# Fifth pair's q' and k' turned by the DMA crossbar, the loads behind them held back, and the first weights gated on an earlier k, in a gated-attention and MLP kernel on one core

## The chip, the cores and the metric

The kernel runs on one core of a Trainium2 chip. The metric is device time in microseconds. A change of 0.5% here is 0.86 us.

The engines are called as in the profile: PE (TensorE; PEld is its weight load), DVE (VectorE), ACT (ScalarE), POOL (GpSimd) and SP (SyncE). SP, ACT and POOL each issue DMAs on a queue of their own; a "q" behind the engine's name (SPq) marks its sequencer.

## The reference

Two layers, one behind the other. The first is a gated linear attention, a recurrence over time for each of 4 x 8 heads of width 48. The second is an MLP on all 3072 tokens.

```python
B, H, S, D = 4, 8, 768, 48
for t in range(S):
    state = alpha[:, :, t, :, None] * state + np.einsum('bhd,bhe->bhde', k[:, :, t], v[:, :, t])
    y[:, :, t] = np.einsum('bhd,bhde->bhe', q[:, :, t], state)
x = y.transpose(0, 2, 1, 3).reshape(B * S, H * D)       # 3072 x 384
h = x @ w_in                                            # 384 -> 2048
g = 0.5 * h * (1.0 + np.tanh(c * (h + 0.044715 * h ** 3)))
out = g @ w_out                                         # 2048 -> 384, float32
```

## The kernel before, in words

**Tiling.** The sequence is cut into 6 chunks of 128 tokens. A unit is one chunk of one batch entry (all 8 heads); two units of one chunk make a pair. There are 12 pairs, numbered 0 to 11 in the order of work (two pairs for each chunk), so the "fifth pair" is pair 4, chunk 2.

**Attention of a pair.** `ln` (ACT) takes the logarithm of alpha, `cum` (PE) sums it along the chunk by a triangular matrix, `b` and `binv` (ACT) are exp of the sum and of its negative. `qp` and `kp` (DVE) scale q and k to q' and k'. Both have to be turned (tokens against features) into the tile `qkT`, called T below. `attn` (PE) forms k' against q', and from pair 4 on also the product of q' with the carried state. `mask` (DVE, four for a pair) keeps the lower triangle, `y` (PE) multiplies by v, `x` (ACT or DVE) copies the result out of PSUM, and x is turned as well, into `xT`. `kv` (PE) and `st` (DVE) carry the state to the next chunk; `rows` and `end` (DVE) prepare its decay.

**Turning.** There are three ways. Pairs 0 to 2 use PE transposes of whole tiles (`t`, L488) and copies out of PSUM (`ev`). The pairs in `ROWS_64` use 32 half-size PE transposes in `turn_halves` (task `t3.0` or `t4.0`, L519) and two DVE or ACT copies of PSUM in `turned_half` (`ev`, L526). The pairs in `TURN_QK` use two DMA transposes through the crossbar that SP issues in `turn_dma` (L546; tasks `turnN.0` for q' and `turnN.1` for k'). From pair 6 on x is turned by SP too (`turn_x_dma`, L552, task `turnN.2`).

**MLP.** `l1m.n` (PE, L684) is an eighth of the first layer for pair m: 6 products of 128x128 by 128x256. `gelu` follows on ACT. `l2m.n` (PE, L703) is a quarter of the second layer for one unit: 4 products with 384 columns. `ot` copies the result out of PSUM, `store` (SP) writes it. PSUM buffers are few: two banks for `yk` (turning, y, kv), four for `ff` (idle products, l1, l2), one pair for `ca`.

**Order.** Every engine runs its instructions in the order in which they were recorded. The first 45 us or so of that order are written out by hand in `FIRST` (P is PE, V DVE, A ACT, G POOL, S SP). The rest is set by a planner (`Scheduler.order`) from its own costs `W` and priorities, nudged by `SHIFT` (priorities) and `AFTER` (extra dependencies). `LANDED` tells the planner when it is to expect the early loads. None of these numbers is a wait in the program; they only decide the order.

**Loads.** The alpha, q and k of pairs 0 and 1 come in twelve loads of one unit each (`RINGS`), numbered load.0 to load.11, on SP's queue, but for those numbered in `BY_ACT`, which ACT issues: load.0 and load.1 are alpha of pair 0 (first and second unit), load.2 and load.3 are q and k of its first unit, load.4 and load.5 q and k of its second. All else is loaded by POOL in the order of `LOADS`: `v0` is v of pair 0, `in 0` to `in 3` the quarters of the first layer's weights, `out n` those of the second, `a6` alpha of pair 6, and a bare number all four of a pair. POOL loads cast to bf16 where needed, and run with several in flight.

**Gates.** A step `gatea 0 1` in `LOADS` is a tiny POOL copy (L343) that reads alpha of pair 0, unit 1, so POOL, and all loads listed behind it, wait until that load has landed. A step `hold k 5` is a POOL copy (L351) that reads T of pair 5, k' half, so the loads behind it wait until the crossbar has delivered it.

```python
def wait(self, r, m, j):
    u = self.p[list(self.p)[m]]
    return lambda e: self.nc.gpsimd.tensor_copy(self.gate[:, 0:1], u[r][:, j, 0, 0:1])
...
t = self.xT[c % self.NX][:, 2 * i + 1, 0, 0:1] if n == "x" else self.p[c, i]["T"][:, "qk".index(n), 0, 0, 0:1]
self.nc.gpsimd.tensor_copy(self.gate[:, 0:1], t)
```

`fill` tasks are products of zeros on PE (L318), put into the opening, seven of them before the first `cum`.

## Time and profile before

| | us |
|---|---|
| time, median of 3 runs | 172.98 (172.68 to 173.5) |
| time of the profiled execution | 173.12 |
| its span | 171.3 |
| outside the span | 1.8 |
| PE busy | 165.6 (97%) |
| ACT busy | 128.8 (75%) |
| DVE busy | 102.8 (60%) |
| POOL busy | 58.8 (34%) |

The page says how much of the span each engine was busy, gives the span in 40 slices, and lists the chain of work that ended last, followed back from the last instruction. The timeline lists instructions in order of time, with the idle time before each and what ended it. The table by windows gives the same for stretches of the span. A source view of one line gives the time from a DMA's issue to its landing. Landing times below are the issue's start plus that.

### The profile page before, as it was taken

The numbers are of one execution on the slowest core, as the hardware profiler recorded it, in microseconds if no ns is written. First come the engines' busy times: TensorE is split into PE (matmuls) and PEld (weight loads), VectorE is DVE, ScalarE is ACT, GpSimd is POOL, SyncE is SP. The second block draws the span as 40 slices with busy tenths as digits, with TensorE's granted clock in tenths as the row PEclk, the third lists the DMA queues.
The fourth block names the chain that finished last, engine by engine and source line by source line (L and its number), as shares of the span: only waits on it lengthen the run. The fifth ranks groups of instructions, "written<-read, shape, count | busy, mean of one in ns | idle before, by whom it ended". The sixth has DMA issues, their size and how long they took to land.

```text
span 171.3 us, 4477 instructions
## 1 busy us (share of the span) xinstructions
PE 165.6 (97%) x1851; PEld 130.3 (76%) x1853; DVE 102.8 (60%) x210; ACT 128.8 (75%) x214; POOL 58.8 (34%) x71
## 2 busy tenths in 40 slices
PE   7889999999999999999999999999999999999993
PEld 2556999666886896796697697797796796886973
DVE  6399940166889999797896798695640825100000
ACT  3568899846979897788798599399798992572831
POOL 2397446997655400096008009402503000000000
PEclk9999999999999999999999999999999999999999
DMA  4999999999999999789998999996799961401102
GB/s 129 308 255 230 204 245 232 226 228 203 214 305 200 236 253 167 97 182 243 216 221 102 211 167 142 236 255 141 208 139 150 126 157 31 138 0 50 46 0 92
DMA packets 53652, 29.91 MB, mean 175 GB/s; under 512 B 41728, under 2 KB 50048, under 8 KB 53632
## 3 DMA queue, kind: packets, MB, share of 16 engines
q0 software_dynamic: 26464, 17.70, 63.0%
q1 hardware_dynamic: 26624, 11.54, 33.8%
q10 hardware_dynamic: 544, 0.39, 0.8%
q8 instruction: 14, 0.23, 0.6%
q14 instruction: 6, 0.05, 0.1%
HBM read 25.17 MB, written 4.72 MB: 174 GB/s over the span
## 4 chain that ended last, share of the span: by engine, by line
PE 91%; DMA 3%; ACT 3%; DVE 1%; issue 0%; DVEq 0%
PE hT L684 37%; PE acc L703 37%; PE at L583 4%; DMA k<-in_k_dram 3%; PE yps L649 2%; PE cum L416 2%; PE kv L600 2%; PE qkT_ps L488 2%; PE yps L563 1%; PE xT_ps L672 1%; PE yps L641 1%; ACT qkT L506 1%; PE k_ps L534 1%; ACT L309 1%; PE qkT_ps L519 1%; PE idle L318 1%
## 5 line engine op out<-in xcount | busy, mean ns | idle before, releaser
L703 PE MATMUL acc<-w_out,gT 128*128 128x384 bf16 (+3 forms) x416 | 68.5, 314 | 0.0
L684 PE MATMUL hT<-xT,w_in 128*128 128x256 bf16 x576 | 67.9, 273 | 0.0
L684 PEld LDWEIGHTS <-w_in 128*128 128x128 bf16 x576 | 61.5, 114 | 1.4
L690 ACT ACTIVATE gT<-hT 128x512 bf16<-128x512 f32 x96 | 54.1, 604 | 5.7 <-PE hT L684 2.6
L703 PEld LDWEIGHTS <-gT 128*128 128x128 bf16 x416 | 37.2, 98 | 20.2
L590 DVE TENSOR_TENSOR atm<-at,ut 128x512 bf16<-128x512 f32 x48 | 30.2, 683 | 6.6 <-PE at L583 6.4
L715 ACT COPY ot<-acc 128x384 f32<-128x384 f32 (+3 forms) x21 | 9.3, 446 | 17.0 <-PE acc L703 16.3
L478 DVE TENSOR_TENSOR kp<-k,binv 128x768 bf16<-128x768 f32 (+1 forms) x15 | 11.9, 795 | 15.6 <-ACT binv L450 14.9
L351 POOL CAST gate<-qkT 128x1 f32<-128x1 bf16 x6 | 1.1, 189 | 50.2 <-DMA qkT<-kp 50.2
L478 DVE TENSOR_TENSOR qp<-q,b 128x768 bf16<-128x768 f32 (+1 forms) x15 | 11.9, 792 | 8.1 <-ACT b L450 8.1
L450 ACT ACTIVATE b<-cum 128x768 f32<-128x768 f32 (+1 forms) x15 | 10.3, 684 | 5.3 <-PE cum L416 3.4
L337 POOL DMA_DIRECT2D k<-in_k_dram x11 | 12.2, 1110 | 5.6 <-DMA vb<-in_v_dram 2.5
L337 POOL DMA_DIRECT2D a<-in_alpha_dram x11 | 12.3, 1117 | 3.5 <-DMA w_in<-in_moe_w_in_dram 1.3
L337 POOL DMA_DIRECT2D vb<-in_v_dram x11 | 12.2, 1109 | 3.7 <-PE hT L684 0.9
L337 POOL DMA_DIRECT2D q<-in_q_dram x11 | 12.2, 1113 | 3.5 <-DMA w_out<-in_moe_w_out_dram 1.0
L466 DVE STREAM_TRANSPOSE rows<-b 32x256 f32<-32x256 f32 x28 | 12.3, 439 | 0.5
L309 ACT ACT_TABLE_LOAD x9 | 11.5, 1283 | 0.9 <-PEq L1059 0.7
L450 ACT ACTIVATE binv<-cum 128x768 bf16<-128x768 f32 (+1 forms) x15 | 10.2, 683 | 2.2 <-PE cum L416 2.1
L690 ACT ACT_TABLE_LOAD x9 | 11.5, 1283 | 0.2
L623 DVE TENSOR_TENSOR stmp<-kv,st 128x384 f32<-128x384 f32 x16 | 8.8, 553 | 1.2 <-PE kv L600 1.1
L626 DVE TENSOR_TENSOR st<-stmp,ends 128x384 bf16<-128x384 f32 x16 | 8.9, 558 | 0.6
L399 ACT ACTIVATE la<-a 128x768 f16<-128x768 f32 (+1 forms) x11 | 8.7, 787 | 0.1
(83 smaller groups left out, 142.7 us busy)
## 6 DMA issues: line engine op xcount, KB each, us to landing
out_dram<-ot SPq DMA_DIRECT2D x19, 192.0 KB, 4.6
a<-in_alpha_dram POOLq DMA_DIRECT2D x9, 384.0 KB, 9.6
q<-in_q_dram POOLq DMA_DIRECT2D x9, 384.0 KB, 8.6
k<-in_k_dram POOLq DMA_DIRECT2D x9, 384.0 KB, 9.2
vb<-in_v_dram POOLq DMA_DIRECT2D x9, 192.0 KB, 9.5
w_in<-in_moe_w_in_dram POOLq DMA_DIRECT2D x4, 384.0 KB, 8.9
w_out<-in_moe_w_out_dram POOLq DMA_DIRECT2D x4, 384.0 KB, 11.1
out_dram<-ot SPq DMA_DIRECT2D x9, 96.0 KB, 5.0
```

The source lines that it names most:

```text
L309: nc.scalar.add_instruction(mybir.InstLoadActFuncSet(name=nc.get_next_instruction_name(), act_func_set_id=i, engine=mybir.EngineType.Activ ...
L337: dma(u[t][:, lo:hi].rearrange("t b h d -> t (b h) d"), src.rearrange("b h s d -> s (b h) d")[c * C:(c + 1) * C])
L450: self.nc.scalar.activation(u[n].rearrange("t i h d -> t i (h d)")[:, lo:hi], cum, AF.Exp, scale=1.0 if n == "b" else -1.0)
L466: nc.vector.transpose(t[f:f + 32], bass.AP(last.tensor, last.offset + o * D + 32 * half, [list(last.ap[0]), [2 * D, H], [1, 32]]))
L478: self.nc.vector.tensor_tensor(out, rows, b, op=ALU.mult)
L590: self.nc.vector.tensor_tensor(u["atm", i][:, o], u["at", i][o], self.ut[:, None, :].to_broadcast([self.C, self.H // 2, self.C]), op=ALU.mult)
L623: nc.vector.tensor_tensor(s, acc, old, op=ALU.add)
L626: nc.vector.tensor_tensor(new.rearrange("f p (o d) -> f (p o) d", o=2), acc.rearrange("f p (o d) -> f (p o) d", o=2), ends, op=ALU.mult)
L684: self.nc.tensor.matmul(h[:, s], w_in[:, j, nt % 4 + s], self.xT[c % self.NX][:, lo:hi, j], start=j == 0, stop=j == self.NKT - 1, skip_gro ...
L690: return lambda e: self.nc.scalar.activation(self.gT[c % self.NG][:, nt:nt + 2, lo * self.C:hi * self.C], f.pop(("h", c, lo, nt)), AF.Gelu ...
L703: self.nc.tensor.matmul(f["acc", c, b][:, lo:hi], self.gT[c % self.NG][:, nt, b * self.C:(b + 1) * self.C], self.w_out[:, nt, lo:hi], star ...
L715: self.copy(e)(f["ot", c, b][:, sl], f["acc", c, b] if half is None else f["acc", c, b, half][:, sl])
```

## The change

Five things are changed, all of them tables; no function is edited.

1. `TURN_QK` takes in pair 4 and `ROWS_64` loses it. Its 32 half-size PE transposes and the two PSUM copies go, and SP issues two DMA transposes for it.
2. `LOADS` gets a `hold k 4` between k and v of pair 5, and `hold k 5` moves ahead of q of pair 7. From pair 5 on, each group of loads stands behind the crossbar's k' of an earlier pair.
3. `gatek 0 1` becomes `gatek 0 0`: the first weights wait for k of the first unit, not of the second.
4. `BY_ACT` loses load.3. That k comes on SP's queue, as its third load.
5. `FIRST`, `LANDED`, `SHIFT`, `AFTER` and the planner's cost of `rows` are written anew, so the order changes on every engine.

```diff
-... zero=..., rows=1400, ...
+... zero=..., rows=1826, ...
-    LOADS = ('gatea 0 1', 'v0', 'gatek 0 1', 'in 0', 'v1', 'in 1', 'in 2', 'in 3', 'out 0', 'out 1', '2a', 'out 2', '2b', 'out 3', '3', '4', '5', '6', 'a7', 'q7', 'hold k 5', 'k7', 'v7', 'a8', 'hold k 6', ...)
+    LOADS = ('gatea 0 1', 'v0', 'gatek 0 0', 'in 0', 'v1', 'in 1', 'in 2', 'in 3', 'out 0', 'out 1', '2a', 'out 2', '2b', 'out 3', '3', '4', 'a5', 'q5', 'k5', 'hold k 4', 'v5', '6', 'a7', 'hold k 5', 'q7', 'k7', 'v7', 'a8', 'hold k 6', ...)
-    BY_ACT = (2, 3,)
+    BY_ACT = (2,)
     FIRST = """
-        A:table.0 A:load.2 A:load.3 S:load.0 S:load.1 S:load.4 A:ln0.0 S:load.5 P:fill.7 P:cum0.0 A:ln0.1 G:gate.0 G:load.12 S:load.6 P:cum0.1 A:b0.0 S:load.7
-        A:bend0.0 V:qp0.0 A:binv0.0 A:binv0.1 S:load.8 V:kp0.0 P:fill.2 P:t0.0 A:b0.1 V:ev0.0 P:fill.1 P:t0.1 S:load.9 A:ev0.1 V:qp0.1 S:load.10 A:bend0.1
-        P:fill.3 P:attn0.0 V:kp0.1 G:gate.1 S:load.11 P:t0.2 G:load.13 V:mask0.0 A:ev0.2 P:t0.3 G:load.14 V:mask0.1 A:ev0.3 P:fill.1 P:t0.4 V:ev0.4 P:fill.1
...
+        S:load.0 A:table.0 A:load.2 S:load.1 A:ln0.0 S:load.3 A:ln0.1 S:load.4 S:load.5 P:fill.7 G:gate.0 G:load.12 S:load.6 S:load.7 S:load.8 P:fill.2
+        P:cum0.0 P:fill.1 A:b0.0 A:bend0.0 P:cum0.1 A:binv0.0 V:qp0.0 A:b0.1 P:t0.0 V:kp0.0 S:load.9 S:load.10 A:bend0.1 A:binv0.1 V:end0.0 P:fill.3 G:gate.1
+        S:load.11 G:load.13 A:ev0.0 P:t0.1 A:ev0.1 V:qp0.1 G:load.14 A:ln1.0 P:fill.1 V:kp0.1 P:fill.1 G:load.15 P:t0.2 P:attn0.0 V:ev0.2 P:t0.3 G:load.16
+        A:ev0.3 P:cum1.0 V:mask0.0 V:mask0.1 P:attn0.1 V:mask0.3 G:load.17 V:mask0.2 A:ln1.1 P:t0.4 A:b1.0 G:load.18 G:load.19 P:cum1.1 P:t0.5 A:binv1.0
+        G:load.20 A:bend1.0 A:ev0.4 A:ev0.5 V:vb0.0 P:fill.1 G:load.21 V:vb0.1 P:y0.0 V:kp1.0 A:x0.0 P:kv0.0 A:b1.1 V:st0.0 P:y0.1 A:x0.1 V:qp1.0 P:tx0.0
+        V:xe0.0 P:t1.1 A:ev1.1 P:t1.0 V:qp1.1 P:fill.1 G:load.22 V:ev1.0 A:bend1.1 A:binv1.1 P:tx0.1 V:end1.0 P:t1.2 V:xe0.1 P:attn1.0 P:l10.0 V:kp1.1
...
-    TURN_QK = (5, 6, 7, 8, 9, 10, 11)
+    TURN_QK = (4, 5, 6, 7, 8, 9, 10, 11)
-    ROWS_64 = (3, 4)
+    ROWS_64 = (3,)
     SHIFT = {
...
     AFTER = {
-        'cum6.0': 'y4.0',
+        'attn10.0': 'l19.2', 'kv5.1': 'kv6.0', 'kv6.0': 'l25.3',
     }
```

Around pairs 4 to 6 the built program's orders, by task, are now these (`...` for what is left out):

```
PE before:   y3.1 cum4.0 ... l13.0-3 t4.0 l13.4-7 attn4.0 l23.0-4 y4.0 l23.5 cum6.0 ... l14.0-5 attn5.0
PE now:      y3.0 l22.3 kv3.0 cum4.0 ... l13.0-6 attn4.0 l13.7 l23.0-3 y4.0 l23.4-6 cum6.0 ... l14.0-6 attn5.0
DVE before:  qp4.0 kp4.0 xe3.0 rows4.0 st3.0 end4.0 qp5.0 kp5.0 ev4.0 ev4.1 rows5.0 end5.0 mask4.0-3
DVE now:     st3.0 x3.1 st3.1 kp4.0 xe3.0 qp4.0 ot2.1 qp5.0 rows5.0 rows4.0 mask4.0-3 end4.0 end5.0 kp5.0
SP before:   store2.0 store2.1 turn5.0 turn5.1 store3.0 turn6.1
SP now:      store2.0 turn4.1 turn4.0 store2.1 turn5.0 turn5.1 store3.0 turn6.0
POOL before: a5 q5 k5 v5 a6 q6 k6 a7 q7 v6 [hold k 5] k7 v7 a8 [hold k 6]
POOL now:    a5 q5 k5 [hold k 4] v5 a6 q6 k6 v6 a7 [hold k 5] q7 k7 v7 a8 [hold k 6]
```

## The prediction

> **What bounds the kernel now.** I read the page first, then the chain that ended last, then the opening and the stretch of pairs 4 and 5 in the timeline, then landing times in the source views.
>
> ```profile
> PE 165.6 (97%) x1851; PEld 130.3 (76%) x1853; DVE 102.8 (60%) x210; ACT 128.8 (75%) x214; POOL 58.8 (34%) x71
> PEclk9999999999999999999999999999999999999999
> ```
>
> PE is the bound, at a full granted clock. From the windows of 10 us (PE busy in the second column after the stretch, the DMA share the last but one):
>
> ```profile
> 0.00:10.00 10.00, 8.04 (x57) 4.13 (x58) 5.65 (x29) 4.69 (x10) 3.81 (x13) 1.00 0.77 228
> 10.00:20.00 10.00, 9.08 (x138) 7.24 (x138) 9.54 (x22) 8.35 (x19) 7.44 (x10) 1.00 1.17 224
> 20.00:30.00 10.00, 10.00 (x107) 9.94 (x106) 3.35 (x7) 9.46 (x18) 5.04 (x7) 1.00 1.21 236
> 60.00:70.00 10.00, 9.98 (x143) 7.64 (x141) 9.02 (x17) 7.98 (x13) 0.00 (x0) 1.00 1.38 202
> ```
>
> From 20 us on PE has next to no idle time. So an end can move in three ways: less PE work, an earlier start of the full stretch (about 16.3 us), or new stalls in it. The chain (start, length, what) has the first two:
>
> ```profile
> 1.92 5.66 DMA k<-in_k_dram
> 7.67 0.57 DVE kp L478
> 8.29 0.40 PE qkT_ps L488 x4
> ...
> 61.01 0.57 PE qkT_ps L519 x32
> ```
>
> In the opening kp of the first unit waits for k, which ACT's queue brings at 7.58. The last line is the fifth pair's turning on PE.
>
> **The change, part by part.** The sum is made against the profiled execution, 173.12 us, which is 0.14 above the median of 172.98.
>
> *1. PE work: -0.57.* The row at 61.01 goes; nothing on PE replaces it. Its two PSUM copies (DVE, 1.28 us from 62.92) go too; DVE is 60% busy and in no long wait of PE, so I count them at 0. The idle products stay 17 in number.
>
> *2. Opening: -0.6.* Nine idle products, not seven, stand before the first cum. They start 0.427 us apart (2.02, 2.45, 2.87 in the rows), so cum starts at 5.04 and not at 4.48. Its seven products took 1.32 us, those of the second unit, at 6.08, 0.82: part of the delay comes back, and it ends near 6.2, not 5.87. Then:
>
> - qp of unit 0 ends near 7.3. kp follows it on DVE at about 7.2 (overlap as in the rows) instead of 7.67, if k has landed by then. The two queues' nearest rows bound that: alpha's second load, issued on SP at 1.52, landed after 4.0 us; q's second, issued at 2.19, after 5.6. For an issue near 2.2 that makes 6.2 to 7.8; I take 7.0, as the third load of the queue lies nearer the second.
> - t0.1 then waits for three idle products: 8.2 instead of 8.29. attn of unit 0 gains 0.1 (9.25 against 9.36).
> - The copies of T of unit 1, both on ACT before (0.48 apart, last end 11.20), are split between DVE and ACT. attn of unit 1 comes at 10.6, not 11.30.
> - The first y waits for v (issued 5.65, landing after 6.8 us; cast on DVE at 12.44), so it stays at 12.85. The gate before v waits for alpha's second load, now without k beside it; 0 to 0.45 earlier, taken as 0.
> - Behind y, ACT had x, vb, b, x, bend, b, ev in a row, 13.34 to 16.29. vb has moved to DVE and one b ahead of x. What is left is a ping-pong over two PSUM banks: x 13.25 to 13.73, second y 13.76, its x to 14.63, t1.1 14.66, its copy (0.585) to 15.67, tx0.1 15.7 to 16.03, xe to 16.4, first product of the MLP at about 16.6, against 17.19: -0.6.
>
> The weights have to keep up. Before, the fourth quarter of w_in (issued 12.33, 10.7 us to landing) came at 23.0 and its first user, l10.6, ran at 23.16: slack 0.16. For the whole 0.6 it must land at 22.55. The gate's copy was at 8.45, the first weight's issue at 8.91; with k at 7.0 the issue comes at about 7.6, 1.3 earlier. How much of it reaches the landing no row shows: between 0 (the DMA share is above 1 from 10 us on) and 1.3 (0.77 in the first 10 us, so there is room). I take 0.7, near the middle, which covers the 0.45 needed.
>
> *3. The new hold.* POOL now stops after k5 until k' of pair 4 has come through the crossbar; queued behind are v5, a6, q6, k6, v6, a7. How long the crossbar takes is in three answers of the source view of L546: the first two turns of pair 5 (loads in flight until 71.2), and the next one, with the load queue empty.
>
> ```profile
> L546 SPq DMA_TRANSPOSE qkT<-qp x1: 1389/1389/1389, 62.2 to 62.2; - x1
> DMA to landing us min/median/max: 7.0/7.0/7.0
> L546 SPq DMA_TRANSPOSE qkT<-kp x1: 2901/2901/2901, 63.7 to 63.7; - x1
> DMA to landing us min/median/max: 9.0/9.0/9.0
> L546 SPq DMA_TRANSPOSE qkT<-kp x1: 1232/1232/1232, 71.9 to 71.9; - x1
> DMA to landing us min/median/max: 2.7/2.7/2.7
> ```
>
> The steps: binv of pair 4 ended at 55.97 and will end near 55.4; kp4 goes first now and ends about 56.3; SP issues the turn at 56.4, behind store2.0. The last load ahead, k5, was issued at 43.47 and landed after 13.6 us, at 57.1, or a little sooner. So the queue is empty and I take the quiet row: 59.2. turn4.0, an issue (1.23) later, lands by 60.5; attn4.0 wants it at 62.4 (64.26, less one l1 of 0.65, less 0.57 and 0.6). No stall.
>
> POOL goes on at 59.7. The first load behind a gate took 5.0 to 6.2 us to land (118.95, 73.06), the next ones about 1.8 more each: v5 65.4, a6 67.2 (66.3 to 68.2), a7 74.4. Before, a6 landed at 60.3 and ln6.0 ran at 66.28, after the last gelu. cum6.0 stood at 69.52 on PE; it is one l2 later now, so 69.52 + 0.65 - 0.57 - 0.6 = 69.0. With ln at 0.84 the limit for a6 is 68.1. Slack 0.9: 0, with up to 0.1 at the late end. The hold costs nothing while the turn is quiet; it has used up nearly eight microseconds of cover, though.
>
> *4. Pair 5's k', next in line.* kp5 now follows the four masks of pair 4 on DVE: attn4.0 ends 63.25, masks 2.48, end, kp 0.95: 66.85, where it was 63.01. Its turn is issued with the lot in flight until 74.4, so 7.0 to 9.0 us apply: 73.9 to 75.9. attn5.0 wants it at 75.3 (75.85 + 0.65 - 0.57 - 0.6). Stall 0 to 0.6; I take 0.15, as the middle lies in front of 75.3. The Trainium skill ("DMA: Bandwidth & Descriptors", "Queues, rings and completion order") says that each DMA engine takes turns between the queues that have work for it, packet by packet; by that rule, with two queues at work, the turn takes about twice the quiet 2.7, lands near 72.3 and stalls nothing, and the sum is -1.17. The two loaded rows are longer than that, and they decide here. The turn of pair 5's k' also opens the next lot (q7 to a8), 2 us later than before (72.72); kp7 has that much to spare.
>
> *5. The rest of the order.* attn7.0, attn8.0 and attn10.0 stand three to six PE steps later, so their turns have more time. The moves of copies between ACT and DVE lie beside PE work: 0.
>
> Sum: -0.57 - 0.6 + 0.15 = -1.02: 172.1 in the profiled execution, 172.0 against the median.
>
> **The rivals.**
>
> *A. The lot comes too late: slower.* Place: ln6.0 and cum6.0. Every microsecond that a6 lands after 68.1 stops PE for one. With the gain of 1.02, the kernel is over 0.86 slower from a stall of 1.9, that is from a turn of pair 4 that takes 5.5 us instead of 2.7 (0.9 of the difference is slack). Rows of 7.0 and 9.0 exist; at 7.0 the stall is 3.4 and the time 175.4, at 5.5 it is 173.9. For it: stores stand on the same queue ahead of it (store2.0 took 8.7 us before, in traffic), and POOL's order is strict. Against it: k5 is down by 57.1, and the turns issued into an empty queue were near 2.7. Centre 174.5.
>
> *B. k and the weights come no sooner: 172.4.* Then the opening keeps only the 0.16 of slack at l10.6. The Trainium skill ("DMA: Bandwidth & Descriptors", "Issuing engines are not separate DMA queues") says that all queues end on the same 16 engines and that spreading issues saves sequencer time alone; by that rule taking k off ACT's queue moves its landing little. As a mechanism of this kernel: the bytes ahead of w_in's fourth quarter are the same, and if the engines were full from the start, it lands at 23.0 again, -0.57 - 0.16 + 0.15. The share of 0.77 in the first 10 us speaks against.
>
> *C. Pair 5's k' is late by 0.75 to 1.5: 172.6 to 173.3.* After the lot's end one turn landed 1.45 later (71.21 to 72.66); with a7 at 74.4 that is 75.85, and each slower load of the lot adds its own delay.
>
> That the turning stays on PE is excluded: the built program has 32 transposes and 32 weight loads less.
>
> **How the numbers follow.** Forecast 0.45 (171.5 to 172.5, centre 172.0), A 0.30, B 0.10, C 0.15. Faster means below 172.1: the better part of the forecast and the early ends of B, 0.40 in all. Slower means above 173.85: A and the tail of C, 0.33. The rest, 0.27, is within 0.5%, about what a measurement of this kernel can tell from no change. The likeliest case alone spans 171.5 to 172.5. The range goes down to 171.3 (v 0.45 earlier, no stall) and up to 175.0, most of A; about 0.18 is left out.
>
> **What the changed profile would show.** Right: no L519 row near 60; the first hT at 16.4 to 16.8 and w_in's fourth quarter down before 22.6; the turn of pair 4's k' landing after about 2.7 us and POOL's gate at about 59; ln6.0 ended before PE reaches cum6.0; no gap ahead of attn5.0 over 0.6. Wrong: a hT that waits for w_in (B), an idle row on PE at cum6.0 released by ln6.0 (A), or at attn5.0 released by a crossbar turn (C), or a gap that I name nowhere, at a place of the new order.

## The result: slower by 8.7%

The changed kernel takes 189.1 us (median of 4 runs, 186.7 to 191.8), the kernel before 172.9 (4 runs, 172.7 to 173.5). The ratio is 1.087, with a 95% interval of 1.082 to 1.092; it leaves out the slowest of the four, 191.8, and by the medians alone it is 1.093. The forecast was 172.0, its range 171.3 to 175.0. The profiled execution took 189.0 us, 15.9 more than the one of before.

The busy line of the page, the granted clock and the DMA share of the changed kernel, in 40 slices:

```profile
PE 170.4 (91%) x1820; PEld 132.5 (71%) x1821; DVE 101.8 (54%) x208; ACT 129.3 (69%) x214; POOL 59.8 (32%) x72
PEclk9999699999999999997999999999858999999999
DMA  5999999999951699997999999999995951330102
```

PE was 97% busy and is 91% busy now. Its clock falls in three places, and from the twelfth slice to the fourteenth (5, 1 and 6 tenths, 51.5 to 65.5 us) the transfer engines have little to do. The two longest waits of PE (total, times, longest, in us):

```profile
PE hT L683 <- DMA xT<-x: 5.2, 1, 5.2
PE at L582 <- DMA qkT<-kp: 3.9, 1, 3.9
```

The chain that ended last (start, length, what) has one transfer for each of three losses, where the chain of before had only k in its opening:

```profile
6.80 9.63 DMA q<-in_q_dram
...
70.70 12.96 DMA qkT<-kp
...
119.21 3.40 PE hT L683 x30
...
126.67 10.43 DMA xT<-x
137.14 5.52 PE hT L683 x30
```

The last line is the clock: 30 products took 3.40 us for pair 7 and 5.52 right behind the wait, for pair 8. The granted clock, by the trace, was 0.50 from 18.6 to 22.0 us, from 83.4 to 86.8 and from 134.6 to 141.4, and 1.00 elsewhere; each stretch begins inside a wait or right behind it. Three windows inside these stretches (the third number from the end is the clock, the second is the DMA share):

```profile
20.00:21.90 1.90, 1.90 (x16) 1.53 (x14) 0.93 (x3) 1.67 (x3) 0.91 (x2) 0.50 1.22 215
83.50:86.80 3.30, 3.08 (x25) 2.13 (x26) 2.44 (x4) 0.60 (x1) 2.20 (x3) 0.50 0.74 188
134.70:141.40 6.70, 4.26 (x21) 2.94 (x21) 0.00 (x0) 1.42 (x3) 0.00 (x0) 0.50 1.46 186
```

And the ten microseconds in which the transfer engines have little to do, before and after:

```profile
50.00:60.00 10.00, 10.00 (x109) 7.56 (x104) 9.82 (x20) 8.46 (x13) 4.60 (x4) 1.00 1.31 226
50.00:60.00 10.00, 10.00 (x141) 7.70 (x139) 8.41 (x17) 9.35 (x16) 0.00 (x0) 1.00 0.46 148
```

Put side by side by the start of the same task on PE, in us, the loss builds up in three steps:

| task | before | after | later by |
|---|---|---|---|
| attn0.0 | 9.36 | 9.02 | -0.34 |
| l10.0, the first hT | 17.19 | 18.39 | 1.20 |
| l11.0 | 24.47 | 27.51 | 3.04 |
| l14.0 | 71.82 | 74.59 | 2.77 |
| l24.0, behind attn5.0 | 77.94 | 85.94 | 8.00 |
| l17.0 | 111.17 | 119.14 | 7.97 |
| l18.0, behind the turn of x of pair 8 | 123.19 | 137.14 | 13.95 |
| l28.0 | 128.87 | 144.88 | 16.01 |
| l211.0 | 163.08 | 179.08 | 16.00 |

So 3.0 are lost in the opening, 5.2 around attn5.0, 8.0 around l18.0. Of the 3.0, 1.2 are there at l10.0, a wait for a load; the other 1.8 are the slow clock, as l10.0 to l11.0 took 9.12 us instead of 7.28.

The source view of the crossbar's line, for the turn of k' of pair 4 and then for that of pair 5:

```profile
L545 SPq DMA_TRANSPOSE qkT<-kp x1: 1335/1335/1335, 61.1 to 61.1; - x1
DMA to landing us min/median/max: 2.8/2.8/2.8
...
L545 SPq DMA_TRANSPOSE qkT<-kp x1: 1316/1316/1316, 70.7 to 70.7; - x1
DMA to landing us min/median/max: 13.0/13.0/13.0
```

For the turn of x of pair 8, which took 10.43 (above), the row of before:

```profile
L552 SPq DMA_TRANSPOSE xT<-x x1: 2142/2142/2142, 112.5 to 112.5; - x1
DMA to landing us min/median/max: 4.8/4.8/4.8
```

And POOL's two gates in its timeline (start, length, idle time before it and what ended that):

```profile
63.94 0.18 POOL L350 CAST gate<-qkT 128x1 f32<-128x1 bf16 x1 [19.52 <-DMA qkT<-kp]
...
84.14 0.18 POOL L350 CAST gate<-qkT 128x1 f32<-128x1 bf16 x1 [12.72 <-DMA qkT<-kp]
```

The new hold lets go at 63.94 and the next lot starts at 84.14, where it started at 72.72.

A warning for what follows: executions of one program with the changed middle scatter by several per cent, in one experiment from 176.5 to 194.6 us. Those of the kernel before, almost fifty over all experiments, lay between 172.2 and 174.4, but for one of 340.6 that nothing here explains. So the total of a single execution says little about differences under some 5 us; the readings rest on rows of the traces. In the experiments, a strip is a POOL load of 128 tokens of a pair (384 KB), a turn is a transpose by the crossbar.

### The profile page after: what moved, and what is told of

The parts are those of the page before. It is cut to its first block, busy times and chain, and to the rows that moved or that the text cites. A ratio compares the mean times of both kernels' runs of the same rounds, so it can differ in the third digit from the quotient of the medians.

```text
span 187.2 us, 4411 instructions
## 1 busy us (share of the span) xinstructions
PE 170.4 (91%) x1820; PEld 132.5 (71%) x1821; DVE 101.8 (54%) x208; ACT 129.3 (69%) x214; POOL 59.8 (32%) x72
## 3 DMA queue, kind: packets, MB, share of 16 engines
HBM read 25.17 MB, written 4.72 MB: 160 GB/s over the span
## 4 chain that ended last, share of the span: by engine, by line
PE 74%; DMA 18%; SPq 3%; ACT 2%; issue 1%; DVE 1%; DVEq 0%
PE hT L683 33%; PE acc L702 30%; DMA qkT<-kp 7%; DMA xT<-x 6%; DMA q<-in_q_dram 5%; SPq L333 3%; PE at L582 3%; PE kv L599 2%; PE yps L648 2%; PE cum L415 1%; PE yps L562 1%; PE qkT_ps L487 1%; ACT L689 1%; PE yps L640 1%; PE xT_ps L671 1%
## 5 line engine op out<-in xcount | busy, mean ns | idle before, releaser
L683 PE MATMUL hT<-xT,w_in 128*128 128x256 bf16 x576 | 72.2, 282 | 5.3 <-DMA xT<-x 5.2
L683 PEld LDWEIGHTS <-w_in 128*128 128x128 bf16 x576 | 62.7, 116 | 9.4 <-issue 5.6
L714 ACT COPY ot<-acc 128x384 f32<-128x384 f32 (+3 forms) x20 | 8.9, 447 | 14.9 <-PE acc L702 14.5
L477 DVE TENSOR_TENSOR qp<-q,b 128x768 bf16<-128x768 f32 (+1 forms) x15 | 11.9, 796 | 12.5 <-ACT b L449 11.4
L477 DVE TENSOR_TENSOR kp<-k,binv 128x768 bf16<-128x768 f32 (+1 forms) x15 | 11.9, 792 | 5.4 <-DMA a<-in_alpha_dram 2.9
L336 POOL DMA_DIRECT2D q<-in_q_dram x11 | 12.2, 1113 | 4.7 <-DMA w_in<-in_moe_w_in_dram 2.1
L336 POOL DMA_DIRECT2D a<-in_alpha_dram x11 | 12.4, 1124 | 2.5 <-DMA w_in<-in_moe_w_in_dram 1.3
L336 POOL DMA_DIRECT2D k<-in_k_dram x11 | 12.2, 1109 | 2.9 <-DMA v<-in_v_dram 1.6
L336 POOL DMA_DIRECT2D vb<-in_v_dram x11 | 12.2, 1111 | 2.7 <-PE hT L683 0.9
L449 ACT ACTIVATE b<-cum 128x768 f32<-128x768 f32 (+1 forms) x15 | 10.2, 682 | 3.5 <-PE cum L415 2.6
L658 DVE CAST x<-yps 128x384 bf16<-128x384 f32 x7 | 3.9, 557 | 15.2 <-PE yps L648 15.2
L582 PE MATMUL at<-qkT 64*128 64x128 bf16 x192 | 8.3, 224 | 3.9 <-DMA qkT<-kp 3.9
L449 ACT ACTIVATE binv<-cum 128x768 bf16<-128x768 f32 (+1 forms) x15 | 10.2, 682 | 0.5 <-PE cum L417 0.5
## 6 DMA issues: line engine op xcount, KB each, us to landing
w_out<-in_moe_w_out_dram POOLq DMA_DIRECT2D x4, 384.0 KB, 11.9
```

The costliest lines, as they stand in the source:

```text
L336: dma(u[t][:, lo:hi].rearrange("t b h d -> t (b h) d"), src.rearrange("b h s d -> s (b h) d")[c * C:(c + 1) * C])
L449: self.nc.scalar.activation(u[n].rearrange("t i h d -> t i (h d)")[:, lo:hi], cum, AF.Exp, scale=1.0 if n == "b" else -1.0)
L477: self.nc.vector.tensor_tensor(out, rows, b, op=ALU.mult)
L582: nc.tensor.matmul(at[o][:, p, :], t[sl, 1, p, :], t[sl, 0, p, :], start=True, stop=True)
L683: self.nc.tensor.matmul(h[:, s], w_in[:, j, nt % 4 + s], self.xT[c % self.NX][:, lo:hi, j], start=j == 0, stop=j == self.NKT - 1, skip_gro ...
L714: self.copy(e)(f["ot", c, b][:, sl], f["acc", c, b] if half is None else f["acc", c, b, half][:, sl])
```

## The experiments: the opening

**The gate alone.** The changed kernel, weights behind k of the second unit again.

```diff
-    LOADS = ('gatea 0 1', 'v0', 'gatek 0 0', 'in 0', ...
+    LOADS = ('gatea 0 1', 'v0', 'gatek 0 1', 'in 0', ...
```

> The changed kernel, but the weights wait for k of the second unit again instead of the first, the one word of the list of loads that the diff altered in the opening; the order on every engine is that of the changed kernel. Theory W (the weights, let go 2 us sooner, fill the transfer engines and the last small loads of the opening, q and k of pair 1, starve): the first weight's issue goes back from 6.9 to about 8.5 to 9, q of pair 1's second unit lands at 12.5 to 14 instead of 16.4, the first hT stands at 16.5 to 17.3 instead of 18.4, and the time falls by 1.5 to 3.5 us, to about 186 to 187.5. Rival S (one more small load at the head of SyncE's queue pushes all those behind it): q of pair 1 still lands at 15.5 or later, the first hT stays beyond 18, and the time stays within 1 us of 189.

**k on ACT's queue.** The changed kernel, its weights still behind k of the first unit.

```diff
-    BY_ACT = (2,)
+    BY_ACT = (2, 3,)
     FIRST = """
-        S:load.0 A:table.0 A:load.2 S:load.1 A:ln0.0 S:load.3 ...
+        S:load.0 A:table.0 A:load.2 A:load.3 S:load.1 A:ln0.0 ...
```

> The changed kernel, but k of the first unit is issued by ACT again, right behind alpha of the first unit; the weights still wait for that k. Theory W: k lands at 7 to 7.6, the weights' issue comes only 0.5 to 0.8 later than in the changed kernel, q of pair 1's second unit lands at 14.5 or later, and the first hT stays near 18: time 188 to 189.5. Rival S: SyncE's queue is as long as in the kernel before, q of pair 1 lands near 13, the first hT at 16.6 to 17.3, time 186 to 187.5.

188.1 and 187.7 us. Source view of the load of q of pair 1's second unit, of the changed kernel and then of the one with the gate put back:

```profile
L333 SPq DMA_DIRECT2D q<-in_q_dram x1: 637/637/637, 6.8 to 6.8; - x1
DMA to landing us min/median/max: 9.6/9.6/9.6
```

```profile
DMA to landing us min/median/max: 5.9/5.9/5.9
```

Both kernels mend the opening: q lands at 12.66 and at 13.54 instead of 16.44, and l11.0 starts at 25.16 and 25.01 instead of 27.51. So neither theory is right alone. The total gains less, 1.0 and 1.4 us: at l14.0 the two kernels are 2.4 and 2.7 ahead of the changed one, but then they wait 4.7 and 4.6 for the T of pair 5 instead of 3.9, and at l28.0 they are 0.9 and 1.3 ahead. The runs with the changed opening put in order by the issue of the first weight show what decides:

| run | first weight issued | q (issued 6.8) lands | l11.0 |
|---|---|---|---|
| the last-lot run | 6.83 | 16.07 | 25.62 |
| opening alone | 6.87 | 16.25 | 27.87 |
| changed kernel | 6.89 | 16.44 | 27.51 |
| k' of pair 5 early | 6.93 | 16.38 | 27.25 |
| holds swapped | 7.01 | 16.32 | 27.60 |
| k on ACT's queue | 7.16 | 13.54 | 25.01 |
| no hold | 7.31 | 13.86 | 25.17 |
| gate alone | 8.28 | 12.66 | 25.16 |
| kernel before (q issued 7.80) | 8.91 | 12.93 | 24.47 |

Where the first weight is issued by 7.01, 0.2 us behind that q, q lands at 16.1 or later; where it is issued at 7.16 or later, by 13.9. The closest pair with one opening are the holds swapped and no hold: 0.30 us apart in the issue, 2.5 in the landing. That the weights crowd it out is how I read this; only the time of issue was varied. Where l11.0 came at 27 or later the clock was at 0.50 for a part of the way; in the last-lot run q was as late, the clock was at 1.00 there, and l11.0 came at 25.62. In no run did the changed opening reach the 24.47 of the kernel before.

**The opening alone**, in the kernel before.

```diff
-    LOADS = ('gatea 0 1', 'v0', 'gatek 0 1', ...       BY_ACT = (2, 3,)
+    LOADS = ('gatea 0 1', 'v0', 'gatek 0 0', ...       BY_ACT = (2,)
     FIRST = """ (that of the changed kernel; behind it the order of the kernel before)
```

> The kernel before with the changed opening alone: the order written out by hand for the first 48 us, k of the first unit on SyncE's queue and the weights behind it, as in the changed kernel; pairs 4 and 5, the holds and the whole order after it are those of the kernel before. If the opening's loss of 3 us passes through to the end (PE has no idle time to swallow it): 175.3 to 176.3, with the first MLP products of chunk 3 some 2.5 to 3.2 us later than before. Rival: the later stages wait for loads and turns that an opening 3 us later lets catch up, so that part of it is swallowed: 173 to 174.5.

177.4, against 172.8 for the kernel before on that chip: 4.6, more than either theory had. l11.0 is 3.4 later, l13.0 4.2 (0.7 of this at pair 3, where the two orders meet), and then nothing comes back: 4.2 at l28.0 and at the end. In the kernel before, then, what the opening loses passes through whole. In the changed kernel it did not, as the totals of 188.1 and 187.7 above show.

## The experiments: the middle

**k' of pair 5 early.** In the changed kernel, on DVE:

```diff
-qp5.0 rows5.0 rows4.0 mask4.0 mask4.1 mask4.2 mask4.3 end4.0 end5.0 kp5.0
+qp5.0 kp5.0 rows5.0 rows4.0 mask4.0 mask4.1 mask4.2 mask4.3 end4.0 end5.0
```

> The changed kernel, but DVE computes k' of pair 5 right behind q' of pair 5, ahead of the rows of pair 5, so that its turn on the crossbar is issued some 3 to 6 us earlier (64.5 to 68 instead of 70.7). Theory M (a crossbar turn and casting loads of POOL that are in flight together slow each other to about a third): the turn is done for the most part before the loads of the lot are in full flight, lands after 3 to 8 us, before 76; the wait of 3.9 us ahead of attn5.0 is under 1 us and the time falls by 3 to 6 us, to about 183 to 186. Rival L (the turn is slow by itself, because of its data or its place in SyncE's queue behind other turns and stores): it takes 10 us or more again, the wait stays at 2 us or more and the time falls by no more than 2 us.

193.3. The turn came at 65.60 and took 8.3 us, so attn5.0 got its T in time, but a6 landed at 74.2 instead of 72.0 and cum6.0 waited 2.5 for ln6.0. The strips of the lot took 7.4 to 12.2 us. A wait moved, and nothing was won: theory M had the place, not the total.

**The holds swapped.**

```diff
-    'k5', 'hold k 4', 'v5', '6', 'a7', 'hold k 5', 'q7', ...
+    'k5', 'hold k 5', 'v5', '6', 'a7', 'hold k 4', 'q7', ...
```

> The changed kernel, but the two holds of pairs 4 and 5 change places in the list of loads: the lot v5 to a7 waits for the turn of k' of pair 5, not of pair 4, so that no load is in flight while that turn runs. Theory M: the turn of k' of pair 5 takes 2.7 to 4 us instead of 13.0 and attn5.0 does not wait for it; in exchange a6 comes some 8 us later, at 80 or beyond, and PE stands still at cum6.0 or at y5.0 (v5): the wait changes its name and its size stays at 3 us or more, time 186 to 193. Rival L: the turn takes 9 us or more with nothing else in flight, and the wait ahead of attn5.0 stays.

198.3. With no load in flight the same turn took 3.5 us (70.79 to 74.30), which ends rival L. In exchange, from the waits of PE:

```profile
PE cum L415 <- ACT la L398: 9.2, 1, 9.2
```

This is my rival A, at its place, with a stall far above the 1.9 to 3.4 that I had given it.

**A hold alone**, in the kernel before, without any turn of pair 4: POOL waits for q' of pair 5 on DVE.

```diff
-    LOADS = (... '4', '5', '6', 'a7', 'q7', 'hold k 5', ...
+    LOADS = (... '4', 'a5', 'q5', 'k5', 'hold p 5', 'v5', '6', 'a7', 'q7', 'hold k 5', ...
+    t = self.p[c, i]["qp"][:, 0, 0, 0:1] if n == "p" else ...
```

> The kernel before with a hold alone: POOL stops after k of pair 5 until q' of pair 5 has been computed (at 62.1 in the kernel before, where the changed kernel's hold let go 2.4 us ahead of attn4.0, as this does), and then issues v5, a6, q6, k6, v6, a7, q7. Pair 4 is turned on PE, k' of pair 5 stands where it stood, no turn is added. Theory H (it is the hold: it leaves the transfer engines empty for 6 to 9 us, and puts the whole lot into the time of pair 5's turns): turns of pair 5 or loads of the lot take 10 us or more, PE waits 3 us or more in all between 65 and 100 us, and the time is 180 to 193. Rival P (the hold is covered, as the prediction had it; the loss comes with the extra turns of pair 4 or with the late k' of pair 5): 173 to 175.

181.3, 8.4 more than before. Its waits of PE:

```profile
PE cum L416 <- ACT la L399: 4.7, 1, 4.7
```

The hold costs this without the crossbar having anything more to do. It is not quite the changed kernel's loss: the lot held back had seven loads, q7 among them, the hold let go at 62.3, both turns of pair 5 ran beside its first strips, and the wait came at cum6.0, as a6 landed at 73.6. Later v7 and a8 took 15.9 and 17.4 us to land beside the turns of pair 6 (7.6 and 13.1).

**No hold**, in the changed kernel: `'hold k 4'` is left out of `LOADS`, POOL issues v5 to a7 right behind k5.

> The changed kernel without the new hold: the lot v5 to a7 is issued right behind k5, as in the kernel before; pair 4 stays on the crossbar and k' of pair 5 stays late, the opening is the changed one. Theory H: the turns of pair 4 now run among loads and take 6 to 9 us instead of 2.8, attn4.0 waits 1.5 to 5 us for them; k' of pair 5 comes after the lot's end and takes under 4 us, with no wait ahead of attn5.0; the later lots come earlier and the wait at xT of chunk 8 is gone: 176.5 to 182. Rival P: attn5.0 still waits 2 us or more and the time stays at 185 or more.

188.5. Waits of PE:

```profile
PE yps L562 <- DMA qkT<-qp: 6.0, 2, 5.8
PE hT L683 <- DMA xT<-x: 5.2, 1, 5.2
```

The turns of pair 4 took 8.5 and 9.6 us among the loads, and PE waited 6.0 for them; the turn of k' of pair 5, now behind the lot, took 2.7, as theory H had it. But the late wait stayed, and the time is one that rival P allowed. The hold is there for a reason: without it the turns of pair 4 come too late.

**The middle alone.** The changed kernel with `FIRST`, `BY_ACT` and the gate of the kernel before.

> The changed kernel with the opening of the kernel before: order by hand for the first 50 us, k of the first unit on ACT's queue, weights behind k of the second unit; the new hold, pair 4 on the crossbar, the late k' of pair 5 and the whole order behind it are those of the changed kernel. If opening and middle add up, this is the changed kernel less what the opening alone cost: 189.1 less 3 to 4.5, that is 184.5 to 186. If the middle's loss hangs on the 3 us by which the opening had moved the stages against the loads: 174 to 180.

184.5 (4 runs, 180.8 to 187.2; profiled execution 181.9). The first products stand where they stood before (17.08). attn5.0 waits 3.6 for k' (68.62 to 81.05, 12.4 us), so the stall is there without the late opening. Opening alone (+4.6) and middle alone (+7.5 to +14, by execution) add up to 12 to 18.5, with the 15.9 between. Of the middle's, 1.2 is a wait at attn3.0 that the changed kernel does not have; it comes from joining the two orders.

**v6 out of the lot.** To the middle alone, this is added:

```diff
-    'hold k 4', 'v5', '6', 'a7', 'hold k 5', 'q7', ...
+    'hold k 4', 'v5', 'a6', 'q6', 'k6', 'a7', 'hold k 5', 'v6', 'q7', ...
```

> The changed kernel with the opening of the kernel before (as in the run of the middle alone, whose median was 184.5 with runs from 180.8 to 187.2), and v6, the cast load that was in flight with the turn of k' of pair 5, moved behind the hold of pair 5: the lot is now v5, a6, q6, k6, a7. Theory Q: the turn of k' of pair 5 lands within 1.5 us of a7, near 76 to 77.5, where it landed at 81.05; attn5.0 waits under 0.6 us instead of 3.6; the next lot opens at 77 to 78 instead of 81.5, and the time falls by 2.5 to 6 us, to 176 to 181. Rival M: with four plain strips in flight the turn still takes 9 us or more, attn5.0 still waits 2.5 us or more, time 181 to 187.

177.7 (4 runs, 174.8 to 180.7); the profiled execution took 177.3, 4.6 less than that of the middle alone. Source view of the turn of k' of pair 5:

```profile
L545 SPq DMA_TRANSPOSE qkT<-kp x1: 1288/1288/1288, 68.8 to 68.8; - x1
DMA to landing us min/median/max: 8.0/8.0/8.0
```

It landed at 76.80, 0.85 after a7, PE did not wait for it at attn5.0, and the next lot opened at 76.92. The time is as theory Q had it. Q's reason (the cast) is tried in the second appendix, below.

## The experiments: what a turn and loads do to each other

Three kernels are the kernel before with an appendix behind its last store, whose transfers are timed by their rows. The first six strips of the first appendix ran beside the kernel's last stores; six strips alone took 13.7 to 13.8 us in all three appendices.

```python
for kinds in ("ssssss", "sTTsssss", "sTTTsssss", "cTTccc", "sssTTsss", "csss1TTcs", "sTcTscs"):   # third appendix
    for x in kinds:
        {"s": strip, "c": cast, "T": turn, "1": lambda: wait(1)}[x]()
    wait()
```

> The kernel before with an appendix behind its last store, whose results go nowhere (its time is that of the kernel before plus the appendix): strips are loads of 128 tokens of a pair, turns are the crossbar's transposes of q' of a pair, each group starting when the one ahead has landed. In order: six strips alone; one turn alone; one turn and six strips started together; two turns alone; six strips and a turn issued when the first strip has landed; four strips on ACT's queue and a turn issued when the first has landed; six strips and then two turns. Theory M (in flight together they slow each other): the turn alone 2.5 to 3 us, six strips alone down about 14 to 16 us after the first issue; with strips in flight the turn takes 6 us or more, and the group as a whole at least 3 us longer than the two after one another would need beyond their overlap, that is longer than six strips alone plus one turn alone. Rival (they share the engines fairly, and a turn's bytes cost no more beside loads than alone): the turn takes 3 to 6 us and the group ends within 1 us of the six strips alone.

> A second appendix behind the last store of the kernel before, whose results go nowhere. Besides the plain strips (f32 to f32) it has cast strips (v, f32 to bf16, as pairs 2 to 11 load it). Groups, each started when the one ahead has landed: six plain strips; a plain strip, a turn issued right behind it, five plain strips; three, a turn, three; four cast strips; a cast strip, a turn right behind it, three cast strips; a cast and three plain strips and, when the first has landed, a turn, then a cast and a plain strip (the lot v5 to a7 of the changed kernel with the turn of k' of pair 5); the same with a plain strip in place of the second cast one. Theory Q (a turn that comes while plain strips stand in the queue waits until they are through, and nothing is slowed; only a turn whose pieces run at the same time as those of a cast strip slows both): groups 2 and 3 end within 2 us of group 1 or with the turn right behind the last strip; group 5 and group 6 take 3 us or more longer than their strips alone; group 7 is 3 us or more shorter than group 6. Rival M (any strip and a turn whose pieces run at the same time slow both): groups 2 and 3 are 3 us or more longer than group 1, and group 7 is as slow as group 6.

> A third appendix behind the last store of the kernel before, whose results go nowhere: s is a plain strip, c a cast strip, T a turn, 1 a wait for the first to land; groups one after another: ssssss, sTTsssss, sTTTsssss, cTTccc, sssTTsss, csss1TTcs, sTcTscs. Theory T (one turn beside strips is only shared time, as the second appendix had it; two or more turns on the queue while strips are in flight make both stall): sTTsssss takes 19 us or more from the first issue to the last landing, where six strips alone take 13.7 and each turn adds 1.1 to 1.5, and at least one of the turns takes 10 us or more; csss1TTcs likewise 18 us or more. Rival (sharing adds up, 1.1 to 2.1 per turn, however many there are, and what slows the kernel's turns is not in this appendix, which has no stores and no engines at work): sTTsssss about 16.5, sTTTsssss about 18, cTTccc about 13, no turn over 9.

| group | first issue to last landing, us | the turns, us |
|---|---|---|
| one turn alone / two alone | 2.7 / 4.1 | 2.7 / 2.7, 2.8 |
| ssssss, T when the first has landed | 13.8 for the strips, 14.6 in all | 7.5 |
| Tssssss | 14.4 | 2.8 |
| four strips on ACT's queue, T when the first has landed | 10.2 | 5.6 |
| sTsssss | 15.0 | 6.7 |
| sssTsss | 14.8 | 7.6 |
| **sTTsssss** | **23.3** | 8.5, 17.1 |
| sssTTsss | 21.0 | 14.1, 16.1 |
| sTTTsssss | 22.2 | 8.6, 18.7, 17.1 |
| **ssssssTT** | 15.3 | 7.4, 6.9 |
| cccc / cTccc / cTTccc | 8.6 / 10.7 / 12.4 | - / 6.4 / 6.4, 7.6 |
| csss1Tcs | 14.1 | 6.0 |
| csss1Tss | 14.5 | 7.6 |
| csss1TTcs | 18.4 | 6.0, 11.7 |
| sTcTscs | 17.2 | 6.9, 11.9 |

Source views of the second appendix (sTsssss) and of the third (the two turns of sTTsssss, one after the other):

```profile
L1071 SPq DMA_TRANSPOSE qkT<-qp x1: 1232/1232/1232, 177.0 to 177.0; - x1
DMA to landing us min/median/max: 6.7/6.7/6.7
```

```profile
L1071 SPq DMA_TRANSPOSE qkT<-qp x1: 1232/1232/1232, 177.2 to 177.2; - x1
DMA to landing us min/median/max: 8.5/8.5/8.5
...
L1071 SPq DMA_TRANSPOSE qkT<-qp x1: 2416/2416/2416, 178.6 to 178.6; - x1
DMA to landing us min/median/max: 17.1/17.1/17.1
```

One turn issued behind strips of POOL takes 6.0 to 7.6 us instead of 2.7 and costs the strips 1 to 2: that is shared time, more than the rival of the first appendix had for the turn and about what it had for the group. M's mutual stall is not there, and Q's cast strip, issued behind the turn as it was here, does nothing special. A second turn adds 4.3 to 8.3 us where plain strips are still issued behind the two; issued behind the last of six strips, with three or four of them still in flight, two turns took 7.4 and 6.9 and added next to nothing. So theory T holds only in part: in the appendices the stall also took strips that come behind the turns.

The changed kernel fits that in part. Up to 75.4 us one turn is beside the lot, and the strips land at 70.22, 72.02, 73.83 and 76.47; at 75.38 the turn of q' of pair 6 joins that of k' of pair 5, and v6 and a7 land at 82.61 and 83.83, 13.5 us after their issue. The source view of line 336, for k6, v6 and a7:

```profile
L336 POOL DMA_DIRECT2D k<-in_k_dram x1: 1151/1151/1151, 68.0 to 68.0; - x1
L336 POOL DMA_DIRECT2D vb<-in_v_dram x1: 1166/1166/1166, 69.1 to 69.1; - x1
L336 POOL DMA_DIRECT2D a<-in_alpha_dram x1: 1182/1182/1182, 70.2 to 70.2; - x1
DMA to landing us min/median/max: 8.5/13.5/13.6
```

No appendix has this order, though: all loads of the lot, the casting v6 among them, were issued before the turn of k' of pair 5 (70.70), and a store and a third turn (k' of pair 6, 78.33) followed. In ssssssTT, the group nearest to it, nothing stalled. So the cast, ahead of the turns, and the stores are not excluded here.

**Turns kept apart.** In the middle alone, a tiny transfer on SP's queue reads the last turn's result, so that the next turn is not issued before that has landed; once for q' of pair 6 only, once for all turns from pair 5 on.

```diff
+            if waits and self.last is not None:
+                self.nc.sync.dma_start(self.seen, self.last)
             self.nc.sync.dma_start_transpose(...)
```

> The run of the middle alone (changed kernel, opening of the kernel before), and one thing more: ahead of the turn of q' of pair 6 SyncE's queue first moves two bytes-pairs of a row of the turned k' of pair 5 into a scratch tile, so that it waits until that turn has landed and the two turns are not on the queue together while the lot v5 to a7 is in flight. Nothing else moves; v6 stays in the lot. Theory T (two turns at once beside strips stall): the lot ends at 76 to 78 instead of 81.1, the turn of k' of pair 5 lands at 76 to 78 instead of 81.05, PE's wait of 3.6 us ahead of attn5.0 is under 1 us, and at the first products of chunk 5's MLP the kernel is 3 us or more ahead of the run of the middle alone; the time falls by 2 to 6 us from a median of 184.5 (best 180.8), to 177 to 181. Rival (the cast load v6 does it, or the stores): turn and lot as late as before, 181 to 187.

> The run of the middle alone with every turn from pair 5 on held, in the same way, until the turn ahead of it on SyncE's queue has landed. Theory T: no turn takes 10 us or more and no strip over 10 us (but for those already in flight ahead of a turn), the waits of PE for turns (3.6 and 1.6 us in the run of the middle alone) are under 1.5 us together, and the time comes to 172.5 to 178; below 172.1 it would beat the kernel before, by the turning that left PE. Against it: each turn of a pair now comes 1.5 to 3 us later where nothing is in flight, and SyncE's stores queue behind the waits: if these decide, new waits stand ahead of attn7.0 to attn10.0 and the time is 178 or more.

189.1 (4 runs, 184.7 to 196.4) and 205.5 (204.7 to 206.1): neither time is mended. In the middle, though, the first run went as theory T has it, but for the end of its lot (80.91): in the profiled execution (196.4) the turn of k' of pair 5 took 8.6 us and landed at 77.57, PE did not wait for it, and l24.0 came at 79.43 and l15.0 at 85.86, against 83.33 and 91.70 in the middle alone. The loss came later: PE waited 9.7 us for q' of pair 9, whose turn took 19.1 beside five loads and the turn of x of pair 8. The longest waits of PE in the second run:

```profile
PE hT L693 <- DMA xT<-x: 9.2, 4, 6.1
PE at L592 <- DMA qkT<-kp: 6.0, 2, 3.7
```

Here the tiny transfers themselves took 2.4 to 6.5 us among the loads, and the turn of k' of pair 5, alone among turns on the queue, was issued at 71.78 and still took 11.2; v6 and a7 took 13.4 and 13.6. Turns kept back met the next lot instead. So a second turn is not needed for the stall. Taking v6 out of the lot and keeping the second turn back each removed the wait at attn5.0; which part of the traffic makes it stays open.

## The experiments: the late loss, and the way back

**The last lot.** The changed kernel with `'hold k 9'` replaced by `'hold x 8'`.

> The changed kernel, but the last-but-one lot (q11, k11, v10) waits for the turn of x of pair 8 instead of that of k' of pair 9; the order on every engine stays. Theory M (a turn and loads in flight together slow each other): the turn of x of pair 8 takes 3 to 6 us instead of 10.4, the wait of 5.2 us at the first product on its xT is under 1 us, PE's clock stays up behind it, and the time falls by 4.5 to 8 us, to 181 to 184.5. Rival: the turn is slow because of the loads already in flight ahead of it and of the stores on its own queue: 8 us or more again, time within 1.5 us of 189; or the lot, being later, makes PE wait at pair 10 or 11 instead.

193.4. The turn of x of pair 8 took 13.8: loads already in flight ahead of it were there, as the rival said, and so was the turn of q' of pair 9 (18.5 us) on its own queue. This run had other collisions from 104 us on (the turns of pair 8 took 14.9 and 12.7), so it does not price the lot.

**The late order of the kernel before**, from l24.0 on (78 us), put behind the run with v6 out of the lot.

> The kernel of the run with v6 behind the hold, with the orders of the kernel before from the second products of chunk 4's second layer on (78 us), where pair 4's turning on PE has no part any more: what stays of the change is pair 4 on the crossbar, the hold for its k' and the moved loads. If the late loss of the run with v6 behind the hold (level with the kernel before at the first products of chunk 5, 4.3 us behind at the end) lies in the changed kernel's late order, this ends within 1 us of the kernel before, 172 to 174. If it lies in the loads, which still come some 5 us later than before, the late waits stay and it ends at 175 to 180.

178.4 (5 runs, 178.0 to 178.5), 1.030 of the kernel before (1.027 to 1.033). The old order does not bring the old time back, but it does take away the loss at l18.0. From l17.0 to l18.0 PE takes 12.0 us in every run with the old late order; with the changed one 14.6 in the run with v6 out of the lot, 18.0 in the changed kernel, and 12.4 to 28.1 over all runs (12.4 in the run with k' early, 12 us behind by then). The rows of the changed kernel say why. PE does y of pair 8 behind l17.4 and no longer ahead of l17.0, so that x is ready to be turned at 123.99 instead of 112.24, 4.9 us behind the start of l17.0 instead of 1.1. On SP's queue that turn now stands behind both turns of pair 9 and two stores, and the issue of one of those turns alone took 4.85 us. It was issued at 126.67 (112.48 before) and took 10.4 (4.8 before). With the old late order, time is lost at another place: l15.0 to l16.0 takes 17.7 us instead of 13.0. How much of the 8.0 is the order and how much the late loads is open, as no run has the changed late order with loads as early as before.

**The hold two loads later**, in the run with v6 out of the lot and in the one with the old late order; one copy of T of pair 3 goes back from DVE to ACT as well, which takes away the wait of 1.2 at attn3.0:

```diff
-    'k5', 'hold k 4', 'v5', 'a6', 'q6', 'k6', 'a7', 'hold k 5', 'v6', ...
+    'k5', 'v5', 'a6', 'hold k 4', 'q6', 'k6', 'a7', 'hold k 5', 'v6', ...
```

> The run with v6 behind the hold of pair 5 (median 177.7, best 174.8), with the new hold two loads later in the list: v5 and a6 are issued right behind k5, and only q6, k6, a7 wait for the turn of k' of pair 4. One copy of T of pair 3 goes back to ACT, where the kernel before had it (1.2 us of PE's wait at attn3.0 came from putting the two orders together). If the loss is the time that the transfer engines lie idle behind the hold, and the late loads that follow from it: v5 and a6 land by 61, the turn of k' of pair 4 still lands by 62.5, the lot of three ends at 71 to 73 instead of 76, the turn of k' of pair 5 lands at 71.5 to 74, the next lot opens there and not at 76.9, and the time is 172 to 175.5. If the late loss comes from the changed order behind pair 5 instead, it stays: 175.5 or more.

> The same two changes made to the run with the order of the kernel before from 78 us on (178.4): the next lot opens 4 us earlier than there, within 1 us of the kernel before (72.7), so that the order of that kernel finds the loads where it had them. If idle transfer engines and late loads are the whole of the middle's and the late loss: 171.8 to 174.0, level with the kernel before or up to 0.6 better for the turning that left PE. If something else in the changed middle costs PE: 175 or more, with a wait of over 2 us between 60 and 100 us.

176.5 to 194.6 (6 runs) with the changed late order; 177.1 (6 runs, 175.8 to 178.7) with the old one, 1.021 of the kernel before (1.016 to 1.025). Up to 86 us the second is level with the kernel before or a little ahead:

| task | before | hold two loads later |
|---|---|---|
| l14.0 | 71.82 | 71.43 |
| k' of pair 5 through the crossbar | 72.66 | 72.70 |
| next lot opens (76.92 with v6 out of the lot alone) | 72.72 | 72.82 |
| l24.0 | 77.94 | 77.70 |
| l15.0 | 85.45 | 85.21 |
| l25.0 | 91.67 | 92.96 |
| l16.0 | 98.46 | 101.75 |

The credit has to be divided. The run with the old late order and the hold in its old place stood at 59.28, 72.31 and 78.57 at l13.0, l14.0 and l24.0; this one stands at 58.42, 71.43 and 77.70. The 0.87 is there at l13.0 already, from the copy of T. So with v6 out of the lot l24.0 was 0.6 behind the kernel before, no more than the wait at attn3.0 had cost; what the place of the hold moves is the opening of the next lot, from 76.9 to 72.8. With the changed late order the profiled execution (194.6) was even 1.4 ahead of the kernel before at l16.0 (97.07) and then lost 3.1 up to l17.0 and 16.1 more up to l18.0. With the old one 3.3 are lost between l15.0 and l16.0, with a wait of PE of 1.9 for the turn of q' at y (L562). The turn of k' of pair 6 ran beside the lot that the hold of pair 5 had just opened (75.17 to 81.72, 6.6 us, against 2.7 before), so the lot behind that one came 6 us later (its last load issued at 84.8, against 78.9), and the turns of pair 7 met it (7.8 and 8.6 us, against 4.5 and 5.1). That chain is read from rows of one execution; no run took it away. No version beat the kernel before.

## Why the prediction was wrong, by its steps

1. **PE work, -0.57: right.** The 32 transposes at L519 are gone (31 instructions less in the records). Between l13.0 and l14.0 PE does the same tasks as before but for them, and with the hold two loads later it takes 13.0 us for them instead of 13.6.

2. **Opening, -0.6: wrong, +3.0.** The steps up to the first y came as forecast or a little sooner: k at 6.29 (7.0), attn of unit 0 at 9.02 (9.25), of unit 1 at 10.42 (10.6), y at 12.47 (12.85). The step that failed is the last one, "first product of the MLP at about 16.6", which came at 18.39. attn1.0 stands ahead of it on PE and needs q of pair 1's second unit, and I had no term for that load: it cost 1.2, and the slow clock behind the wait 1.8. I had worked out what the earlier gate does for the weights and not what the weights do to the twelve small loads that they now ran beside. The 0.7 that I gave the weights was wrong as well: issued 2.0 us earlier, the fourth quarter landed at 22.97 against 23.00. Rival B was right in that and too small in its price, since it left the small loads out too.

3. **The new hold, 0: right in the row that I watched, wrong in what it costs.** The queue was empty, the turn of k' of pair 4 took 2.8, attn4.0 did not wait, and a6 was down at 72.02 in a kernel 3 us late, with no wait at cum6.0. But I priced the hold at its first user alone. The sentence that the hold "has used up nearly eight microseconds of cover" had the cost in it, and I gave it no term: the lot of six loads moved into the time of the turns of pairs 5 and 6, and every lot behind it as well. A hold alone, with q7 in its lot too, cost 8.4 in the one execution there is. With v6 out of the lot the loss up to l24.0 was 0.6 to 0.9, and with the hold two loads later the next lot opened on time as well.

4. **k' of pair 5, +0.15: the mechanism was right, the sizes off.** It was issued among the lot's loads, as forecast, but took 13.0 and not 7.0 to 9.0, and the wait came to 3.9 and, with the slow clock behind it, to 5.2. The two rows of before were turns at the tail of a lot; here two more turns and a store followed it onto the queue while the lot was in flight. Which of these, or the cast of v6, made it longer is open. Rival C had the place at a third of the price. The Trainium skill ("DMA: Bandwidth & Descriptors", "Queues, rings and completion order") says that each DMA engine takes turns between the queues that have work, packet by packet; by it the turn would have taken about twice 2.7, and the prediction set that aside for its two rows, rightly. One turn beside strips took 6.0 to 7.6 in the appendices, not far from the rule; two with strips issued behind them took up to 18.7, which it does not give.

5. **The rest of the order, 0: wrong, +8.0.** The step that failed is that attn7.0, attn8.0 and attn10.0 stand later on PE, "so their turns have more time". That holds for the turns ahead of them. What stands behind attn8.0 got less: y of pair 8 came later against l17.0, and the turn of its x, issued behind both turns of pair 9, took 10.4 us beside loads and stores; that is the "gap that I name nowhere", 5.2 of wait and 2.1 of slow clock. I had looked at the orders of PE ahead of the turns and not at what x would meet on SP's queue. With the old late order this loss was gone in every run, and the late lots cost 3 to 5 us at l15.0 to l16.0 instead; the shares of order and late lots are open.

Rival A, at 0.30, did not happen in this kernel, but it is what the holds swapped (9.2), the hold alone (4.7) and k' early (2.5) turned the loss into. I read it and C as two ends of one debt, the transfers that were not made between 52 and 65 us; no run shows that they trade one for one.

## What to carry to other kernels

A hold in a load queue must be priced at every load behind it and at every other transfer that the delayed lot will then meet, not at the first user alone; here the wait in the middle went when one load was taken out of the lot, and the next lot came on time when two loads were moved ahead of the hold. The quiet row of a crossbar turn (2.7) is a price only where no load is in flight; beside loads look at what is issued behind the turn as well. When a task moves later in the order of one engine, look at what its result must still pass through, here the queue in front of the turn of x. Before small loads are crowded by large ones, look which of them stands next on the critical engine: 0.30 us in the time of issue went with 2.5 us in the landing.

## What the runs showed of the hardware

- One turn issued behind strips took 6.0 to 7.6 us instead of 2.7, and six strips 1.1 to 1.3 longer than 13.7. Two turns with strips issued behind them: 21.0 to 23.3 for the group, 6 to 8 more than with one; two turns behind the last strip: 15.3. Beside cast strips alone the second turn added 1.7. Why some of these groups stall was not found, and in the kernel a turn with no other on its queue took 11.2.
- The granted clock of PE was 0.50 for 3.4 us in the opening, for 3.4 at attn5.0 and for 6.8 at l18.0, each time at or behind a wait of PE (1.2, 3.9 and 5.2 us), and 1.00 elsewhere. This cost 1.3 to 2.1 us beyond each wait (30 products in 5.52 instead of 3.40).
- Executions of one program in which turns and lots overlap spread by up to 10% (176.5 to 194.6), where the kernel before ran between 172.2 and 174.4, but for the one of 340.6.
